# Taking GpSimd out of the first layer's weight conversions, and reordering the loads of weight pieces and alpha, in a retention and two-layer kernel

## The chip, the cores and the metric

The kernel runs on one core of one Trainium2 chip. The metric is the time of one execution in microseconds (us); the median of three runs before the change is 808.59. The engines are called PE (TensorE, the matmuls), PEld (its weight loads), DVE (VectorE), ACT (ScalarE), POOL (GpSimd) and SP (SyncE, which issues the DMAs). L12 is line 12 of the kernel before.

## What is computed

Four batches of 576 tokens pass through a retention with 8 heads of 64 (an attention without softmax, with a decay per head), then through two gated layers:

```python
ret = (q @ k.T / 8) * gamma**(i - j) * (i >= j)        # per head
x = concat_heads(ret @ v)                              # 2304 tokens x 512
h = ((x @ w1) * (x @ w2)) @ w3                         # 512 -> 1024 -> 1024
y = h @ moe_w_out                                      # 1024 -> 512
h = y @ w_in                                           # 512 -> 2048
g = maximum(h, 0) + alpha * minimum(h, 0)              # alpha: one per column of h
out = g @ moe2_w_out                                   # 2048 -> 512
```

The weights of the layers arrive as float64 bits and are converted in the kernel.

## The kernel before

**Numbers.** Each operand of a product is split into a high half (rounded to the matmul's type, by ACT) and a low half (the rest, by a DVE subtraction). A product is then three matmuls: high by high, high by low, low by high.

**A weight piece** (`Weights`, L60 to L144) is 128 x 512 numbers of 64 bits, 512 KB. `_first` makes two ACT passes (L94, L95), `_second` four DVE operations in a row (L104, L105, L107, L109), `_third` the high half (L115), `_fourth` the low half (L123). The subclass `Pieces` (L853) puts `_fourth` on POOL (L858).

**Products** of the first layer, of g and of the output are made by a seven-product scheme for 2 x 2 blocks, so each weight and each third of the tokens also needs sums and differences of its blocks. For the weights w1 and w2 these are four sums of 128 x 256 per column block c (`AbUnits.sums`, L544; for c = 0 on DVE, for the seven others on POOL), for the tokens four subtractions of 128 x 768 (`x_operands`, L599, its `less` in L616; `ab_operands` hands them to POOL), for w_out2 four subtractions of 128 x 256 per pair of pieces (`Operands.add`, L262, its `less` in L271 on POOL). Here the pieces of w_out2 are also multiplied by a sign per row that comes from alpha (`signed`, L287, POOL).

**Stages, in order.**

- *Attention*: one batch is five chunks. Batch 0 runs in two halves, then L707 to L711 lists, step by step, what conversion goes beside which chunk; batches 1 to 3 are 15 links of a chain (L742), and the table `beside` (L724) tells what is put beside each. The order of DVE and POOL is the program's here (L662 to L748), elsewhere a scheduler orders those two; PE, ACT and SP follow the program throughout. `ready` (L674) scales q on POOL (L361, L363) and k on ACT (L354); scores are multiplied by the decay mask on DVE (L388), the state is updated on DVE (L407) and decayed on POOL (L411), and ACT copies the result (L447).
- *Loads of the start* (L649 to L661): SP issues the constants, the pairs of heads of batch 0, and then, between the pairs of batch 1, weight pieces 0 and 1 (`abu.load`). `load_batch(2)` and then piece 2 and 3 (`abu.load(4)`) follow at L712, `load_batch(3)` beside link 4. A raw piece lies in one of three buffers. Alpha is loaded at L831, behind all of it, and L833 to L837 make the sign and its products on DVE.
- *First layer* (L916 to L996): 24 groups, a column block by a third of the tokens, of seven products of six matmuls. Per group ACT copies PSUM four times (L795, L799, L803, L807), DVE reads PSUM three times (L812, L817, L823) and multiplies (L824). A product is often added into a bank that ACT or DVE must have read first. Beside them `at` (L921) places, by group and position a, b or c: the units of w1 and w2, the first ten pieces of w_out1 and w3 (`ws_tick`, spread by `WS`), and pairs of w_out2 (`ops2.tick`, from `OPS0` at `OPS1` tenths), four of eight here (`PAIRS_IN_X`).
- *Fold* (L1027): w3 by w_out1 in 192 matmuls, with the other 14 pieces of these two weights converted beside it.
- *y*: 576 matmuls; w_in is converted beside it, all on DVE and ACT.
- *g* (L1472): 32 groups, a column block by a third of the tokens, as in the first layer but without the units of w1 and w2; the other four pairs of w_out2 are converted at the places listed in `spots` (L1463).
- *Output* (L1577): 18 blocks' worth of seven products each.

Of the kernel before, what the change touches and what calls it, by code (L numbers as in the profile page):

```python
# [12 lines left out]
ALU = mybir.AluOpType  # L13
# [17 lines left out]
WS, OPS0, OPS1 = 24, 43, 10  # L31


def _f32(ap):
    return ap.bitcast(F32)
# [112 lines left out]
def retention_moe_kernel(ctx: ExitStack, tc, qk, kv, w_out1, w3t, w12, w_in, w_out2, alpha, c_row, c_pair, out):  # L148
# [61 lines left out]
    class Operands:  # L210
# [37 lines left out]
        def hi(self, j, u, src):  # L248
            self.u[j, u] = self.places(j, u)
            for h, _, x in self.halves(j, u, src):  # L250
                nc.scalar.copy(h, x)

        def lo(self, j, u, src):
            for h, l, x in self.halves(j, u, src):
                nc.vector.tensor_tensor(out=l, in0=x, in1=_f32(h), op=ALU.subtract)  # L255
            t = self.u.pop((j, u))
            if j != self.stays:
                for n, op in enumerate(self.PLACES[u]):
                    nc.sync.dma_start(out=wod[WOPS.index(op)][:, j].rearrange("p (h w) -> p h w", h=2),
                                      in_=_f32(t[:, n]))  # L260

        def add(self, j, at, steps, ahead=None):  # L262
# [7 lines left out]
            def less(out, a, b):  # L270
                nc.gpsimd.tensor_tensor(out=out, in0=a, in1=b, op=ALU.subtract)  # L271

            def sums1():
                a, b = w.ab[x][0], w.ab[y][0]
                t[1] = self.sum_room(f"t1_{j}").bitcast(F32)
                less(t[1][:, lower], a[:, upper], a[:, lower])
                less(t[1][:, upper], b[:, upper], t[1][:, lower])

            def sums3():
                a, b = w.ab[x][0], w.ab[y][0]  # L280
                t[3] = self.sum_room(f"t3_{j}").bitcast(F32)
                less(t[3][:, lower], b[:, upper], a[:, upper])
                less(t[3][:, upper], b[:, lower], t[1][:, upper])

            def signed(i):
                a = w.ab[i][0]
                nc.gpsimd.tensor_tensor(out=a, in0=a, in1=sg[:, i:i + 1].to_broadcast([P, 512]), op=ALU.mult)  # L287
# [5 lines left out]
                "h1": lambda: self.hi(j, "u1", w.ab[x][0][:, lower]),  # L293
                "l1": lambda: self.lo(j, "u1", w.ab[x][0][:, lower]),
                "h2": lambda: self.hi(j, "u2", w.ab[y][0]), "l2": lambda: self.lo(j, "u2", w.ab[y][0]),
                "t1": sums1, "t3": sums3,
                "h3": lambda: self.hi(j, "u3", t[1]), "l3": lambda: self.lo(j, "u3", t[1]),
                "h4": lambda: self.hi(j, "u4", t[3]), "l4": lambda: self.lo(j, "u4", t[3]),
# [215 lines left out]
    class AbUnits:  # L514
# [203 lines left out]
    def to_xr():  # L718
# [112 lines left out]
    nc.sync.dma_start(out=al, in_=alpha)  # L831

    nc.vector.tensor_scalar(out=sg, in0=al, scalar1=1.0, scalar2=-2.0, op0=ALU.is_gt, op1=ALU.mult)  # L833
    nc.vector.tensor_scalar(out=sg, in0=sg, scalar1=1.0, scalar2=None, op0=ALU.add)
    nc.vector.tensor_tensor(out=sal, in0=sg, in1=al, op=ALU.mult)
    pairs = sg.rearrange("p (j r) -> p j r", r=2)
    nc.vector.tensor_tensor(out=both, in0=pairs[:, :, 0], in1=pairs[:, :, 1], op=ALU.mult)  # L837

    PRE, PAIRS_IN_X = 10, 4
# [116 lines left out]
    at(13, "b", lambda: [ops2.load(i) for i in range(2)])  # L956
# [494 lines left out]
    def come():  # L1451
# [215 lines left out]
```

## Time and profile before

| | us |
|---|---|
| median of 3 runs (806.4 to 809.1) | 808.59 |
| the profiled execution | 807.9 |
| its span, first to last instruction | 806.1 |
| PE busy in the span | 753.7 |
| DVE busy | 649.3 |
| ACT busy | 422.7 |
| POOL busy | 164.2 |
| TensorE's granted clock, mean share of full | 0.981 |

An engine's busy time is the union of its instructions. A matmul's end is modelled, so a busy PE is not PE at its best. The idle time in front of an instruction is put down to what released it last. Of POOL the profile's spans are rough.

### The profile page before, as it was taken

What the parts mean: (1) busy time and instruction counts of PE and PEld (TensorE: products, weight loads), DVE (VectorE), ACT (ScalarE), POOL (GpSimd) and SP (SyncE); (2) the same over time, 40 slices, a digit from 0 to 9 for tenths busy, and PEclk for the clock granted to TensorE, in tenths of its full rate; (3) what the DMA queues carried; (4) which work ended last, traced back from release to release, by engine and by line L of the source; (5) the groups of instructions that cost most, each with busy time, mean ns of one, the idle gap of its engine ahead of it and who ended that gap; (6) DMA issues with size and microseconds to landing.
All of it is one profiled execution on the core that took longest, in us unless ns stands there. A gap on an engine that the chain in (4) does not pass through costs nothing.

```text
span 806.1 us, 13426 instructions
## 1 busy us (share of the span) xinstructions
PE 753.7 (93%) x4979; PEld 701.8 (87%) x4979; DVE 649.3 (81%) x966; ACT 422.7 (52%) x750; POOL 164.2 (20%) x149
## 2 busy tenths in 40 slices
PE   9665899998989989899999999999999999999998
PEld 5555789887988988799999999999999888888887
DVE  4856997999699896989999576979876688777874
ACT  3443465566455553466676554556644454444443
POOL 2344751332245342400000020212010000000000
PEclk9878999999999999999999999999999999999999
DMA  9936014677565696558784698575899944444440
GB/s 355 383 100 229 2 53 164 203 239 253 205 209 186 228 408 242 195 189 320 256 284 165 222 316 318 184 262 193 273 332 348 307 131 131 132 142 132 142 132 27
DMA packets 106849, 173.26 MB, mean 215 GB/s; under 512 B 8096, under 2 KB 73888, under 8 KB 106784
## 3 DMA queue, kind: packets, MB, share of 16 engines
q1 hardware_dynamic: 106784, 172.40, 62.1%
q8 instruction: 39, 0.64, 0.3%
q14 instruction: 26, 0.21, 0.1%
HBM read 112.34 MB, written 60.03 MB: 214 GB/s over the span
## 4 chain that ended last, share of the span: by engine, by line
PE 56%; DVE 11%; DMA 4%; issue 3%; ACT 1%; POOL 0%; SPq 0%; DVEq 0%; ACTq 0%; POOLq 0%
PE h L772 23%; PE o L1379 14%; PE y L1195 12%; PE o L1381 7%; DMA cells<-gd 2%; DVE a L107 2%; DVE a L109 1%; DMA abd<-xs 1%; DVE a L104 1%; DMA raww<-in_w3t_dram 1%; DVE xs L107 1%; DVE xs L255 1%; PE pw L1035 1%; DVE a L105 1%; DVE xs L824 1%
## 5 line engine op out<-in xcount | busy, mean ns | idle before, releaser
L1195 PE MATMUL y<-yab,wa 128*128 128x384 f32 x576 | 100.2, 334 | 0.0
L1195 PEld LDWEIGHTS y<-yab,wa 128*128 128x128 f32 x576 | 99.8, 188 | 0.3 <-DVE yab L1017 0.2
L1360 DVE TENSOR_TENSOR cells<-cells,cells 128x1024 fp32r<-128x1024 f32 x63 | 76.3, 1221 | 26.7 <-ACT cells L1354 26.6
L1379 PE MATMUL o<-wa,cells 128*128 128x512 f32 x288 | 76.6, 393 | 0.0
L1354 ACT CAST cells<-cells 128x1024 fp32r<-128x1024 f32 x63 | 64.9, 1053 | 7.0 <-DVE cells L1347 4.2
L772 PE MATMUL h<-xl,wa 128*128 128x384 f32 x288 | 55.6, 339 | 3.9 <-DVE xs L812 2.3
L1379 PEld LDWEIGHTS o<-wa,cells 128*128 128x128 f32 x288 | 51.4, 189 | 8.5
L1379 PE MATMUL o<-wop,cells 128*128 128x512 f32 x216 | 57.0, 392 | 1.0 <-DVE cells L1391 1.0
L772 PE MATMUL h<-xT,wa 128*128 128x384 f32 x288 | 55.8, 335 | 0.8 <-DVE g L1258 0.7
L772 PE MATMUL h<-xB,wa 128*128 128x384 f32 x288 | 56.5, 334 | 0.0
L772 PE MATMUL h<-wa 128*128 128x384 f32 x264 | 51.4, 343 | 4.8 <-DVE xs L812 2.6
L772 PEld LDWEIGHTS h<-xl,wa 128*128 128x128 f32 x288 | 51.2, 191 | 5.2 <-DVE xs L812 3.0
L287 POOL TENSOR_TENSOR a<-a,al 128x512 f32<-128x512 f32 x8 | 8.8, 1099 | 219.3 <-DVE a L109 219.3
L772 PEld LDWEIGHTS h<-wa 128*128 128x128 f32 x264 | 47.1, 192 | 6.0 <-DVE xs L812 3.2
L772 PE MATMUL h<-xr,wa 128*128 128x384 f32 x240 | 46.9, 341 | 5.1 <-DVE xs L812 3.2
L772 PEld LDWEIGHTS h<-xT,wa 128*128 128x128 f32 x288 | 50.3, 188 | 1.4 <-DVE g L1258 1.4
L772 PEld LDWEIGHTS h<-xB,wa 128*128 128x128 f32 x288 | 50.5, 188 | 0.0
L772 PEld LDWEIGHTS h<-xr,wa 128*128 128x128 f32 x240 | 42.5, 191 | 6.3 <-DVE xs L812 3.9
L1379 PEld LDWEIGHTS o<-wop,cells 128*128 128x128 f32 x216 | 39.4, 188 | 8.9 <-issue 1.2
L109 DVE CUSTOM_DVE_ANT_0 a<-a,b 128x1024 uint16<-128x1024 uint16 x54 | 44.3, 822 | 1.8
L1381 PEld LDWEIGHTS o<-wa,cells 128*128 128x128 f32 x288 | 41.8, 190 | 3.5
L1381 PE MATMUL o<-wa,cells 128*128 128x256 f32 x288 | 44.5, 282 | 0.0
(232 smaller groups left out, 1677.4 us busy)
## 6 DMA issues: line engine op xcount, KB each, us to landing
gd<-g SPq DMA_DIRECT2D x96, 192.0 KB, 4.2
cells<-gd SPq DMA_DIRECT2D x36, 512.0 KB, 6.0
abd<-xs SPq DMA_DIRECT2D x24, 384.0 KB, 3.4
yf<-abd SPq DMA_DIRECT2D x24, 384.0 KB, 6.3
rawi<-in_w_in_dram SPq DMA_DIRECT2D x16, 512.0 KB, 5.7
wod<-xs SPq DMA_DIRECT2D x28, 256.0 KB, 4.0
xs<-in_w_out_dram SPq DMA_DIRECT2D x12, 512.0 KB, 4.9
wa<-wod SPq DMA_DIRECT2D x12, 512.0 KB, 6.4
```

Of the source, the lines that this page charges most:

```text
L104: nc.vector.tensor_scalar(out=a, in0=a, scalar1=self.LEAST, scalar2=self.MOST, op0=ALU.max, op1=ALU.min)
L105: nc.vector.tensor_scalar(out=ai, in0=ai, scalar1=5, scalar2=2, op0=ALU.logical_shift_left, op1=ALU.logical_shift_right)
L107: nc.vector.scalar_tensor_tensor(out=ai, in0=upper, scalar=0xC0000000, in1=ai, op0=ALU.bitwise_and, op1=ALU.bitwise_or)
L109: nc.vector.tensor_tensor(out=a.bitcast(I32), in0=a.bitcast(I32), in1=b, op=ALU.add)
L255: nc.vector.tensor_tensor(out=l, in0=x, in1=_f32(h), op=ALU.subtract)
L287: nc.gpsimd.tensor_tensor(out=a, in0=a, in1=sg[:, i:i + 1].to_broadcast([P, 512]), op=ALU.mult)
L772: nc.tensor.matmul(ps, a[:, x, ks], b[:, y, k], start=(fresh and n == 0), stop=(n == 5), skip_group_check=True)
L1195: nc.tensor.matmul(ys[o], wpc[c][a][:, oc], yab[u][:, bb, c % 2], start=(c == 0 and i == 0), stop=(c == C1 - 1 and i == 2))
L1354: nc.scalar.copy(h.bitcast(F32R), self.q[name])
L1360: nc.vector.tensor_tensor(out=l.bitcast(F32R), in0=q[name], in1=h, op=ALU.subtract)
L1379: nc.tensor.matmul(ps, h[:, k], w[k], start=(fresh and k == 0), stop=(k == C1 - 1), skip_group_check=True)
L1381: nc.tensor.matmul(ps[:, 256:], l[:, k], w[k][:, 0:256], start=False, stop=(k == C1 - 1), skip_group_check=True)
```

## The change

The first layer's POOL work goes to DVE: the sums of w1 and w2, the subtractions of the tokens' blocks for all three thirds, the low halves of w_out1 and w3 (in the fold too), and the subtractions of w_out2. For the pairs of w_out2 that are converted there, the sign is not multiplied in first; it is a scale of the ACT pass and a scalar of the DVE operation. In g these steps stay on POOL, with the sign multiplied as before. Three pairs of w_out2 are converted in the first layer and five in g. Pieces 0 and 1 are loaded ahead of batch 1, alpha and piece 2 behind batch 1 and ahead of batch 2. The steps beside the chunks and links move, and the operations on alpha come beside link 1.

```diff
-WS, OPS0, OPS1 = 24, 43, 10
+WS, OPS0, OPS1 = 29, 49, 10
...
-        def hi(self, j, u, src):
+        def hi(self, j, u, src, sign=None):
             self.u[j, u] = self.places(j, u)
             for h, _, x in self.halves(j, u, src):
-                nc.scalar.copy(h, x)
+                if sign is None:
+                    nc.scalar.copy(h, x)
+                else:
+                    nc.scalar.activation(h, x, AF.Copy, scale=sign)
...
+                    nc.vector.scalar_tensor_tensor(out=l, in0=x, scalar=sign, in1=_f32(h), op0=ALU.mult,
+                                                   op1=ALU.subtract)
...
-            def less(out, a, b):
-                nc.gpsimd.tensor_tensor(out=out, in0=a, in1=b, op=ALU.subtract)
+            late = not self.small
+            sx, sy, sxy = (sg[:, x:x + 1], sg[:, y:y + 1], both[:, j:j + 1]) if late else (None, None, None)
+
+            def less(out, a, b, sign=None):
+                if sign is not None:
+                    nc.vector.scalar_tensor_tensor(out=out, in0=a, scalar=sign, in1=b, op0=ALU.mult, op1=ALU.subtract)
+                else:
+                    (nc.vector if late else nc.gpsimd).tensor_tensor(out=out, in0=a, in1=b, op=ALU.subtract)
...
             def signed(i):
                 a = w.ab[i][0]
-                nc.gpsimd.tensor_tensor(out=a, in0=a, in1=sg[:, i:i + 1].to_broadcast([P, 512]), op=ALU.mult)
+                if not late:
+                    nc.gpsimd.tensor_tensor(out=a, in0=a, in1=sg[:, i:i + 1].to_broadcast([P, 512]), op=ALU.mult)
...
-            engine = nc.vector if c == 0 else nc.gpsimd
+            engine = nc.vector
...
-        return x_operands(p, place, in_sums, nc.gpsimd)
+        return x_operands(p, place, in_sums)
...
-    load_pair(1, 0)
-    abu.load(1)
-    load_pair(1, 1)
-    load_pair(1, 2)
     abu.load(2)
-    load_pair(1, 3)
+    load_batch(1)
+    nc.sync.dma_start(out=al, in_=alpha)
+    abu.load(3)
...
+    def signs():
+        nc.vector.tensor_scalar(out=sg, in0=al, scalar1=1.0, scalar2=-2.0, op0=ALU.is_gt, op1=ALU.mult)
+        nc.vector.tensor_scalar(out=sg, in0=sg, scalar1=1.0, scalar2=None, op0=ALU.add)
+        nc.vector.tensor_tensor(out=sal, in0=sg, in1=al, op=ALU.mult)
+        pairs = sg.rearrange("p (j r) -> p j r", r=2)
+        nc.vector.tensor_tensor(out=both, in0=pairs[:, :, 0], in1=pairs[:, :, 1], op=ALU.mult)
...
-                 ab_steps(0, "f0"), s1[2], ready(rs[1], 0), ab_steps(0, "s0"), s1[3], ready(rs[1], 1), ab_steps(0, "h0 f1"),
-                 s1[4], ready(rs[1], 2), ab_steps(0, "s1 l0"), s1[5], ready(rs[1], 3), ab_steps(0, "h1")):
+                 ab_steps(0, "f0"), s1[2], ab_steps(0, "f1"), s1[3], ready(rs[1], 0), ab_steps(0, "s0"), s1[4],
+                 ready(rs[1], 1), ab_steps(0, "s1 h0"), s1[5], ready(rs[1], 2), ready(rs[1], 3),
+                 ab_steps(0, "l0 h1")):
...
-        0: [ab_steps(0, "l2"), ab_steps(1, "f0")],
-        1: [ready(rs[2], 0), ab_steps(1, "s0")],
-        2: [ready(rs[2], 1), lambda: make.extend(ab_operands(0)), x_steps(1), ab_steps(1, "f1")],
-        3: [ready(rs[2], 2), ready(rs[2], 3, nc.vector), x_steps(1)],
-        4: [lambda: load_batch(3), ab_steps(1, "s1")],
-        5: [x_steps(2)],
+        0: [ab_steps(0, "l2")],
+        1: [signs, ab_steps(1, "f0")],
+        2: [ready(rs[2], 0), lambda: make.extend(ab_operands(0)), x_steps(1), ab_steps(1, "s0")],
+        3: [ready(rs[2], 1), ready(rs[2], 2), ready(rs[2], 3, nc.vector), x_steps(1)],
+        4: [lambda: load_batch(3), ab_steps(1, "f1"), x_steps(1)],
+        5: [x_steps(1), ab_steps(1, "s1")],
...
-    nc.sync.dma_start(out=al, in_=alpha)
...
-    PRE, PAIRS_IN_X = 10, 4
+    PRE, PAIRS_IN_X = 10, 3
...
-        def _fourth(self, i):
-            hi, lo = self.dest.pop(i)
-            nc.gpsimd.tensor_tensor(out=lo, in0=self.ab.pop(i)[0], in1=_f32(hi), op=ALU.subtract)
...
-    spots = ("2a 2b 2c 3a 3b 3c 4a 4b 5a 5b", "8c 9a 9b 9c 10a 10b 10c 11a 11b 11c",
-             "12c 13a 13b 13c 14a 14b 14c 15a 15b 15c", "17c 18a 18c 19a 19c 20a 20b 20c")
+    spots = ("1a 1b 1c 2a 2b 2c 3a 3b 3c 4a", "5a 5b 5c 6a 6b 6c 7a 7b 7c 8a", "9a 9b 9c 10a 10b 10c 11a 11b 11c 12a",
+             "13a 13b 13c 14a 14b 14c 15a 15b 16a 16b", "17b 17c 18a 18c 19b 19c 20b 20c")
```

## Rows read from the trace of the kernel before

**Rows 1.** Busy time of each engine (instructions) by stage, granted clock, DMA

```profile
core 0: us, PE busy (x) PEld busy (x) DVE busy (x) ACT busy (x) POOL busy (x), PEclk, DMA share, GB/s
102.50:301.00 198.50, 182.32 (x1011) 177.50 (x1011) 174.37 (x279) 114.60 (x228) 76.04 (x65) 0.98 0.62 214
301.10:347.50 46.40, 44.21 (x195) 35.98 (x194) 37.36 (x51) 22.67 (x41) 16.79 (x12) 1.00 0.57 203
447.50:622.80 175.30, 173.93 (x998) 172.68 (x997) 134.64 (x219) 95.94 (x175) 24.28 (x24) 1.00 0.81 278
...
0.00:33.00 33.00, 25.70 (x306) 16.07 (x310) 18.25 (x35) 12.77 (x29) 9.38 (x15) 0.97 0.96 358
347.50:447.50 100.00, 100.00 (x578) 99.78 (x577) 93.48 (x165) 65.55 (x116) 0.00 (x0) 1.00 0.68 244
```

**Rows 2.** Waits of PE over the span: us in total, times, longest

```profile
PE h L772 <- DVE xs L812: 9.5, 8, 3.0
PE h L772 <- ACT h L795: 5.7, 4, 2.3
...
PE h L772 <- DVE g L1258: 1.3, 2, 0.7
...
PE pw L1035 <- ACT wa L115: 1.4, 1, 1.4
...
PE pw L1035 <- POOL wa L858: 0.8, 1, 0.8
```

**Rows 3.** Timeline at PE's longest wait of the first layer: start, us, engine, line

```profile
293.85 1.66 POOL L858 TENSOR_TENSOR xl<-a,xl 128x512 fp32r<-128x512 f32 x1 [5.55 <-ACT xl L115]
294.30 1.76 DVE L109 CUSTOM_DVE_ANT_0 a<-a,b 128x1024 uint16<-128x1024 uint16 x1
...
297.38 2.29 PE L772 MATMUL h<-xr,wa 128*128 128x384 f32 x6 [3.00 <-DVE xs L812]
```

**Rows 4.** First layer, DVE and POOL by form: busy us, mean ns

```profile
L824 DVE TENSOR_TENSOR xs<-xs 128x384 f32<-128x384 f32 x23 | 18.7, 813 | 0.1
...
L542 DVE TENSOR_TENSOR wa<-xs,wa 128x512 fp32r<-128x512 f32 x9 | 6.7, 749 | 0.0
...
L616 POOL TENSOR_TENSOR xs<-xs 128x768 f32<-128x768 f32 x5 | 10.6, 2118 | 6.8 <-DVE xl L612 3.9 <-DVE xr L612 2.8
```

**Rows 5.** The same list in the y stage; last, one L824 in the fold's list

```profile
L107 DVE SCALAR_TENSOR_TENSOR a<-rawi,a 128x512 uint32<-128x512 uint32 x16 | 10.9, 689 | 0.3
L109 DVE CUSTOM_DVE_ANT_0 a<-a,b 128x1024 uint16<-128x1024 uint16 x16 | 10.9, 686 | 0.0
L104 DVE TENSOR_SCALAR a<-a 128x512 f32<-128x512 f32 x16 | 6.7, 422 | 1.3 <-ACT a L94 1.1
...
L1149 DVE TENSOR_TENSOR wa<-s,wa 128x512 fp32r<-128x512 f32 x8 | 5.3, 689 | 0.8 <-ACT wa L1143 0.7
...
L1133 DVE TENSOR_TENSOR s<-a 128x256 f32<-128x256 f32 x8 | 3.4, 422 | 0.2
...
L616 DVE TENSOR_TENSOR t_T<-xs 128x768 f32<-128x768 f32 x3 | 2.9, 953 | 0.0
...
L824 DVE TENSOR_TENSOR xs<-xs 128x384 f32<-128x384 f32 x1 | 0.5, 546 | 0.0
```

**Rows 6.** Timeline of the attention, six instructions behind or after its waits

```profile
32.88 0.49 PE L426 MATMUL o<-heads_r,heads_l 64*64 64x64 f32 x8 [2.70 <-ACT xs L447]
...
47.28 0.66 ACT L94 ACTIVATE a<-raw 128x512 f32<-128x512 f32 x1 [8.82 <-DMA raw<-in_w_dram]
...
49.03 0.91 PE L426 MATMUL o<-heads_l 64*64 64x128 f32 x10 [6.98 <-ACT xs L447]
...
59.07 1.16 PE L384 MATMUL sc<-heads_r 64*128 64x128 f32 x16
...
76.41 0.18 DVE L833 TENSOR_SCALAR al<-al 128x16 f32<-128x16 f32 x1 [5.78 <-DMA al<-in_alpha_dram]
...
77.77 1.97 PE L435 MATMUL o<-heads_l,heads_r 128*64 128x128 f32 x16 [3.40 <-DVE heads_l L388]
```

More of the change, by code (lines that the diff above doesn't have):

```diff
@@ L245, in halves, with lo @@
             return [(t[:, :, 0], t[:, :, 1], src)]
-        def hi(self, j, u, src):
+        def hi(self, j, u, src, sign=None):
             self.u[j, u] = self.places(j, u)
             for h, _, x in self.halves(j, u, src):
-                nc.scalar.copy(h, x)
-        def lo(self, j, u, src):
-            for h, l, x in self.halves(j, u, src):
-                nc.vector.tensor_tensor(out=l, in0=x, in1=_f32(h), op=ALU.subtract)
+                if sign is None:
+                    nc.scalar.copy(h, x)
+                else:
+                    nc.scalar.activation(h, x, AF.Copy, scale=sign)
+        def lo(self, j, u, src, sign=None):
+            for h, l, x in self.halves(j, u, src):
+                if sign is None:
+                    nc.vector.tensor_tensor(out=l, in0=x, in1=_f32(h), op=ALU.subtract)
+                else:
+                    nc.vector.scalar_tensor_tensor(out=l, in0=x, scalar=sign, in1=_f32(h), op0=ALU.mult,
+                                                   op1=ALU.subtract)
             t = self.u.pop((j, u))
@@ L267, in add @@
             t = {}
-            def less(out, a, b):
-                nc.gpsimd.tensor_tensor(out=out, in0=a, in1=b, op=ALU.subtract)
+            late = not self.small
[3 more added lines that the diff above has]
+                    nc.vector.scalar_tensor_tensor(out=out, in0=a, scalar=sign, in1=b, op0=ALU.mult, op1=ALU.subtract)
+                else:
+                    (nc.vector if late else nc.gpsimd).tensor_tensor(out=out, in0=a, in1=b, op=ALU.subtract)
             def sums1():
@@ L276, in sums1 @@
                 less(t[1][:, lower], a[:, upper], a[:, lower])
-                less(t[1][:, upper], b[:, upper], t[1][:, lower])
+                less(t[1][:, upper], b[:, upper], t[1][:, lower], sxy)
             def sums3():
@@ L281, in sums3 @@
                 t[3] = self.sum_room(f"t3_{j}").bitcast(F32)
-                less(t[3][:, lower], b[:, upper], a[:, upper])
-                less(t[3][:, upper], b[:, lower], t[1][:, upper])
+                less(t[3][:, lower], b[:, upper], a[:, upper], sxy)
+                less(t[3][:, upper], b[:, lower], t[1][:, upper], sxy)
             def signed(i):
                 a = w.ab[i][0]
-                nc.gpsimd.tensor_tensor(out=a, in0=a, in1=sg[:, i:i + 1].to_broadcast([P, 512]), op=ALU.mult)
+                if not late:
+                    nc.gpsimd.tensor_tensor(out=a, in0=a, in1=sg[:, i:i + 1].to_broadcast([P, 512]), op=ALU.mult)
             parts = {
@@ L292, in add @@
                 "sx": lambda: w._second(x), "sy": lambda: w._second(y),
-                "h1": lambda: self.hi(j, "u1", w.ab[x][0][:, lower]),
-                "l1": lambda: self.lo(j, "u1", w.ab[x][0][:, lower]),
-                "h2": lambda: self.hi(j, "u2", w.ab[y][0]), "l2": lambda: self.lo(j, "u2", w.ab[y][0]),
+                "h1": lambda: self.hi(j, "u1", w.ab[x][0][:, lower], sx),
+                "l1": lambda: self.lo(j, "u1", w.ab[x][0][:, lower], sx),
+                "h2": lambda: self.hi(j, "u2", w.ab[y][0], sy), "l2": lambda: self.lo(j, "u2", w.ab[y][0], sy),
                 "t1": sums1, "t3": sums3,
-                "h3": lambda: self.hi(j, "u3", t[1]), "l3": lambda: self.lo(j, "u3", t[1]),
-                "h4": lambda: self.hi(j, "u4", t[3]), "l4": lambda: self.lo(j, "u4", t[3]),
+                "h3": lambda: self.hi(j, "u3", t[1], sx), "l3": lambda: self.lo(j, "u3", t[1], sx),
+                "h4": lambda: self.hi(j, "u4", t[3], sx), "l4": lambda: self.lo(j, "u4", t[3], sx),
                 "x": lambda: self.load(x + 2), "y": lambda: self.load(y + 2),
@@ L828, in spill @@
             nc.sync.dma_start(out=abd[self.p][:, self.j], in_=self.f)
-    nc.sync.dma_start(out=al, in_=alpha)
[L833 to L837, printed above, removed]
-    PRE, PAIRS_IN_X = 10, 4
+    PRE, PAIRS_IN_X = 10, 3
     fs_raw, fs_a, fs_b = Ring(xs, 12, 4, 4), Ring(xs, 28, 2, 3), Ring(xs, 40, 2, 2)
@@ L955, in retention_moe_kernel @@
         at(m // 3, "abc"[m % 3], ws_tick)
-    at(13, "b", lambda: [ops2.load(i) for i in range(2)])
+    at(15, "b", lambda: [ops2.load(i) for i in range(2)])
     for n in range(7 * PAIRS_IN_X + 1):
```

## The prediction

> **What bounds the kernel now.** I read the stretches first [rows 1]: the attention up to 102.5 us, the first layer (24 groups of 42 matmuls) from 102.5 to 301, the fold of the two weights, then y, the second layer g and the output blocks. g does the same 1008 matmuls as the first layer and takes 175.3 us with TensorE (PE) all but gapless; the first layer takes 198.5. So 23.2 us of the first layer are no matmul time. In y PE never stops either. Time can be won only ahead of 347.5 us: in the attention, the first layer and the fold.
>
> Then the waits of PE [rows 2]. In the first layer they end on two things: VectorE's (DVE) L812, which must have read a PSUM bank before the next product may be added into it, and ScalarE's (ACT) copy L795. Those two make 15.2 us; the rest of the 23.2 is matmuls just after a wait and the clock, which the stretch grants at 0.98 of full against 1.00 in g [rows 1]. L812 itself is short; it is late because DVE works in order behind conversions of weights.
>
> The timeline at the longest of these waits shows why DVE is late [rows 3]: an L109 that starts beside a GpSimd (POOL) operation takes 1.76 us, and PE then idles 3.00. In y, where POOL does nothing, the same L109 takes 0.686 [rows 5]. The list by form tells it for the whole stretch [rows 4]: L824 takes 0.813 on the mean, against 0.546 for one in the fold with no POOL beside it, L542 0.749 against 0.689 for the like L1149 [rows 5]. Subtracting the price of the y stretch, 13 such groups (L824 with 6.1 the largest, L542 with 0.5 among the smallest) were lengthened by 32.5 us together, out of DVE's 174.4 busy [rows 1]. POOL was busy 76.0 there, so each of its microseconds cost DVE 0.43.
>
> In the attention three waits have nothing to do with POOL [rows 6]. ACT stands 8.82 us before L94 of the third weight piece, whose load is queued behind the whole third batch, and PE idles 6.98 behind it. DVE stands 5.78 us before L833 for alpha, queued last of all, and PE idles 3.40. An earlier piece, queued between the pairs of the second batch, leaves PE idle 2.70.
>
> **The change, part by part. First layer.** All POOL work of this stretch goes. DVE gets 24 sums of 128x256 at 0.422 (10.1 us), 5 subtractions L616 at 0.953 (4.8), 12 low halves (the former L858) at 0.689 like L1149 (8.3) and, for three pairs of w_out2, 12 subtractions at 0.422 (5.0): 28.2 us [rows 5]. The 8 multiplications by the sign (L287) vanish: the sign rides in operations that are there anyway, DVE's with a scalar operand at the price of their kind (L107 is one), ACT's as a scale. The fourth pair leaves for g: two conversions at 2 x 0.422 + 0.689 + 0.686 = 2.22, three low halves at 0.689 and one at 0.422: 6.9 less. DVE then has 174.4 - 32.5 + 28.2 - 6.9 = 163.2 us to do. Whether PE waits depends on how full DVE is. It was 174.4/198.5 = 88% full; at the same fullness 163.2 us need 185.8, so the stretch **gains 12.7**. Bounds: 23.2 (no wait left, g's length) and, with PE's waits as frequent as now, 0. I take 12.7, as the same four readers of PSUM per group must still squeeze between conversions. What stands late next is the L812 behind the sums, now four more DVE instructions in a row.
>
> **Attention.** The SP queue now issues two pieces (six DMAs) ahead of the second batch, alpha and the third piece (three DMAs) behind it and ahead of the third. Up to 33 us the queue runs at 358 GB/s [rows 1], so two pieces of 0.52 MB put the first pair of the second batch back by 2.9 us, the middle two by half of it, the last by nothing, since as many bytes stand before it as did. PE needs all four pairs for its next batch, so the 2.70 shrinks by 1.0 at most. The third piece now costs the third batch the 1.5 us that it waited itself: that batch is there by about the time at which the piece came, 47.3, and its first scores now start at 59.07 [rows 6], so some 10 us are free before this load is the next thing late. The waits for piece and alpha go: 6.98 + 3.40 + 1.0 = 11.4. The small operations on alpha move into the ordered part (0.7 us of DVE, like L833). Against it, DVE takes 7 subtractions of 0.953 and 4 sums of 0.422 from POOL, 8.4 us, and gets back 0.43 of the POOL time removed: 7 x 2.12 [rows 4] and 4 of about half of that, 19 us, so 8.2. POOL keeps the scaling and the decay of the states, so stretching does not end there. I take **9** of the 11.4, leaving 2.4 for these and for the order by hand; bounds 0 (the third batch or DVE sets the same pace) and 14.
>
> **Fold.** DVE takes the low halves here too. A piece costs it 2.22 + 0.689 = 2.91 us uncontended [rows 5] and POOL's step leaves the chain. The two waits of PE, 1.4 and 0.8, go [rows 2]: **2.2**; bounds 0 and 46.4 - 44.0 = 2.4.
>
> **g.** A fifth pair is converted here: two loads, seven stores, 10 ACT, 12 DVE and 6 POOL operations, about 7 us of DVE in a stretch where it is busy 134.6 of 175.3 [rows 1]. PE covers it. The steps now also lie where one third of the tokens follows the last, around which both waits of PE (1.3 us for two) lie today [rows 2]. I charge 0.5; bounds 0 and 4 (three such places at 1.3).
>
> **Sum**: 9 + 12.7 + 2.2 - 0.5 = 23.4. The profiled execution spans 806.1 and took 807.9, so 782.7 and 784.5; the median, 808.6, is 0.7 above it: 785. About 0.3% (2.4 us) is what a measurement here can tell from no change.
>
> **Rivals.** *DVE becomes the bound, slower.* If the long rows are not POOL's doing but DMA traffic's or the order's, DVE keeps its 32.5: 174.4 + 28.2 - 6.9 = 195.7, at 88% a stretch of 222.9, 24 us longer, which the 11 of attention and fold do not pay: about 822. It turns slower in this stretch once under 21.3 of the 32.5 come back. For it: DVE is the fullest helper, and L812 behind a queue is the present wait. Against it: y, with DVE 93% busy and POOL at 0, has every price at its minimum [rows 1, 5], and the long ones of rows 3 lie beside POOL. The Trainium skill speaks for it: "Perfetto Trace Analysis", section Optimizing Scalar/DVE Operations, says that where DVE is saturated, handing work to ScalarE or even GpSimd may make sense, and this change does the reverse; the same sentence adds that the two share a read port, so that the hand-over might not help, and the 1.76 beside 0.686 sides with that addition. Chance 0.06.
>
> *Half of it.* Waits shift rather than vanish: the third and fourth batches' loads set the pace of the attention (gain 3) and the four sums in a row keep L812 late (gain 5 in the first layer): 806.1 - 3 - 5 - 2 + 1.8 + 0.7 and 1 for g, about 800. For it: DVE stays 88% full either way. Against: the waits listed sit at the stretched operations. Chance 0.18.
>
> *No effect.* The critical waits are only re-dealt, within 0.3%. For it: PE's slack downstream is nil, but upstream any later load may take over. Chance 0.04.
>
> The forecast, with gains of 15 to 36, has 0.72. Its best case, 14 + 20 + 2, gives 772. The range reaches from there to 800, into the half case, and leaves out about 0.2. **Faster** 0.72 + 0.18 = 0.90, same 0.04, slower 0.06.
>
> **What would show it.** Right: no POOL work between the first group and y; L824 near 0.55 and L109 near 0.69 in every stretch; the first layer about 186 long, its waits for L812 and L795 under 8 us; L94 of the third piece without its 8.82, no wait for alpha, first group near 93.5; g still near 175. Wrong: L824 or L109 still long with POOL idle (then the first rival); DVE over 95% busy in the first layer with more waits for L812; a wait of DVE or ACT for the third batch's loads as long as the one that went; g beyond 178.

## The result, and the profile after

The changed kernel takes 779.02 us (median of 4 runs, 777.58 to 780.67) beside 808.85 for the kernel before on the same chip: a ratio of 0.963, 95% interval 0.960 to 0.967. Forecast were 785 and a range of 772 to 800. The profiled execution took 780.34, its span is 778.6. All lines below are those of the changed kernel; L792 is the former L772, L832 and L844 the former L812 and L824, L815 the former L795. One correction to the text ahead: g has 24 groups, not 32, and the output 9 blocks, not 18; no number rests on these counts.

The windows by stage, columns as in [rows 1]:

```profile
core 0: us, PE busy (x) PEld busy (x) DVE busy (x) ACT busy (x) POOL busy (x), PEclk, DMA share, GB/s
0.00:33.00 33.00, 27.08 (x330) 17.97 (x334) 19.51 (x37) 13.77 (x31) 10.13 (x16) 0.94 0.97 361
33.00:91.50 58.50, 47.43 (x853) 41.29 (x853) 54.95 (x77) 29.00 (x56) 20.81 (x22) 0.86 0.46 171
91.50:271.00 179.50, 177.03 (x1015) 175.07 (x1012) 158.15 (x317) 110.77 (x218) 0.00 (x0) 1.00 0.64 216
271.10:314.60 43.50, 43.50 (x193) 35.99 (x192) 36.02 (x68) 24.78 (x42) 0.00 (x0) 1.00 0.68 247
314.60:414.50 99.90, 99.90 (x578) 99.88 (x577) 92.10 (x163) 65.36 (x116) 0.00 (x0) 1.00 0.67 239
414.50:596.10 181.60, 176.33 (x998) 174.16 (x997) 138.85 (x231) 99.18 (x183) 28.93 (x30) 0.99 0.81 284
```

Subtracted from [rows 1]: the first layer is 19.2 us shorter (198.6 to 179.4, taken between its first and last matmul), the attention 10.8 (102.5 to 91.7), the fold 2.8; y and the output are the same within 0.8; g is 6.3 longer (175.3 to 181.6). POOL stands at 0 from 91.5 to 414.5, PE fills the first layer at a clock of 1.00, and the only place that lost is g.

The list by form of the first layer, to be held against [rows 4] and [rows 5]:

```profile
L837 DVE TENSOR_TENSOR xs<-h,xs 128x384 f32<-128x384 f32 x24 | 13.3, 555 | 12.5 <-PE h L792 12.3
L832 DVE TENSOR_TENSOR xs<-h,xs 128x384 f32<-128x384 f32 x24 | 13.3, 553 | 4.3 <-PE h L792 4.3
L844 DVE TENSOR_TENSOR xs<-xs 128x384 f32<-128x384 f32 x23 | 12.7, 552 | 0.0
...
L109 DVE CUSTOM_DVE_ANT_0 xs<-xs 128x1024 uint16<-128x1024 uint16 x16 | 11.0, 686 | 0.8
...
L109 DVE CUSTOM_DVE_ANT_0 a<-a,b 128x1024 uint16<-128x1024 uint16 x14 | 9.6, 685 | 0.0
...
L123 DVE TENSOR_TENSOR xs<-xs 128x512 fp32r<-128x512 f32 x10 | 6.9, 686 | 0.0
...
L261 DVE SCALAR_TENSOR_TENSOR xs<-xs,al 128x512 fp32r<-128x512 f32 x9 | 6.6, 745 | 1.4 <-ACT xs L254 1.4
```

Every operation that y has too is at y's price again, L109 at 0.686, and the multiplication L844 at 0.552 where it was 0.813. (L261, new in this stretch and with a scalar per row, costs 0.745.) DVE idles 16.8 us in front of L832 and L837 waiting for PE; that is nothing new, before it was 15.0 for the same two operations:

```profile
L817 DVE TENSOR_TENSOR xs<-h,xs 128x384 f32<-128x384 f32 x24 | 13.3, 553 | 11.3 <-PE h L772 11.1
L812 DVE TENSOR_TENSOR xs<-h,xs 128x384 f32<-128x384 f32 x24 | 13.2, 550 | 3.7 <-PE h L772 3.7
```

PE's own waits in this stretch were 15.2 us for L812 and L795 [rows 2]; by the timeline these three are left, 2.5 together:

```profile
143.75 2.37 PE L792 MATMUL h<-xr,wa 128*128 128x384 f32 x12 [0.26 <-ACT h L815]
217.89 2.38 PE L792 MATMUL h<-xl,wa 128*128 128x384 f32 x12 [0.47 <-ACT h L815]
268.84 1.32 PE L792 MATMUL h<-xr,wa 128*128 128x384 f32 x6 [1.74 <-DVE xs L832]
```

In the attention, no wait for the load of the third piece or of alpha is left: L94 of that piece starts without one at 39.88, and so does the first operation on alpha at 40.4. The timelines of ACT and, for g, of ACT and PE:

```profile
39.88 0.68 ACT L94 ACTIVATE a<-raw 128x512 f32<-128x512 f32 x1
...
455.80 0.66 ACT L94 ACTIVATE a<-rawo 128x512 f32<-128x512 f32 x1 [5.13 <-DMA rawo<-in_w_out_dram]
```

```profile
457.56 1.31 PE L792 MATMUL h<-xT,wa 128*128 128x384 f32 x6 [0.27 <-ACT u L1273]
460.71 1.31 PE L792 MATMUL h<-xT,wv 128*128 128x384 f32 x6 [1.84 <-ACT h L1278]
469.11 1.33 PE L792 MATMUL h<-xT,wv 128*128 128x384 f32 x6 [0.84 <-ACT h L1278]
495.57 1.31 PE L792 MATMUL h<-xT,wa 128*128 128x384 f32 x6 [2.01 <-DVE g L1266]
```

A raw piece of g's second pair is what is late now: ACT stands 5.13 before it, ACT's copies behind it come late, and PE waits. PE's waits in g are 5.3 us where they were 1.3; the rest of the 6.3 is matmul time (busy 176.33 beside 173.93), part of it at a lower clock: 0.70 of full from 496 to 498 and 0.50 (the lower of its two levels, 1.2 GHz) from 498 to 500, right behind the last of the four.

### The profile page after: what moved, and what is told of

Its sections match the earlier page's. It is cut to its first block, busy times and chain, and to the rows that moved or that the text cites. A ratio compares the mean times of both kernels' runs of the same rounds, so it can differ in the third digit from the quotient of the medians.

```text
span 778.6 us, 13360 instructions
## 1 busy us (share of the span) xinstructions
PE 750.1 (96%) x4977; PEld 701.6 (90%) x4979; DVE 638.2 (82%) x1042; ACT 424.0 (54%) x750; POOL 59.9 (8%) x67
## 5 line engine op out<-in xcount | busy, mean ns | idle before, releaser
L792 PE MATMUL h<-xT,wa 128*128 128x384 f32 x288 | 55.8, 335 | 2.3 <-DVE g L1266 2.0
L792 PE MATMUL h<-xB,wa 128*128 128x384 f32 x288 | 57.4, 338 | 0.0
L792 PE MATMUL h<-xl,wa 128*128 128x384 f32 x288 | 54.9, 336 | 0.5 <-ACT h L815 0.5
L792 PEld LDWEIGHTS h<-xT,wa 128*128 128x128 f32 x288 | 50.3, 188 | 2.9 <-DVE g L1266 2.3
L792 PEld LDWEIGHTS h<-xl,wa 128*128 128x128 f32 x288 | 50.1, 188 | 1.5 <-ACT h L815 1.4
L792 PEld LDWEIGHTS h<-xB,wa 128*128 128x128 f32 x288 | 51.2, 190 | 0.0
L792 PE MATMUL h<-wa 128*128 128x384 f32 x264 | 49.7, 335 | 0.0
L792 PE MATMUL h<-xr,wa 128*128 128x384 f32 x240 | 45.7, 335 | 2.0 <-DVE xs L832 1.7
L792 PEld LDWEIGHTS h<-wa 128*128 128x128 f32 x264 | 46.0, 188 | 0.3 <-ACT h L815 0.2
L301 POOL TENSOR_TENSOR a<-a,al 128x512 f32<-128x512 f32 x10 | 11.1, 1113 | 444.0 <-DVE a L109 444.0
L792 PEld LDWEIGHTS h<-xr,wa 128*128 128x128 f32 x240 | 41.9, 188 | 2.6 <-DVE xs L832 2.1
L1259 DVE SCALAR_TENSOR_TENSOR g<-h,al,g 128x384 f32<-128x384 f32 x48 | 29.2, 611 | 14.1 <-ACT g L1257 12.0
## 6 DMA issues: line engine op xcount, KB each, us to landing
gd<-g SPq DMA_DIRECT2D x96, 192.0 KB, 4.1
```

Source lines behind the costliest of these rows:

```text
L792: nc.tensor.matmul(ps, a[:, x, ks], b[:, y, k], start=(fresh and n == 0), stop=(n == 5), skip_group_check=True)
L1259: nc.vector.scalar_tensor_tensor(out=g, in0=ps, scalar=sal[:, c], in1=g, op0=ALU.mult, op1=ALU.max)
```

## Experiments

The change has three parts: loads and order of the attention, POOL's work to DVE, and the fourth pair's move with a wider spread of the steps. The first four runs take them apart. Stage lengths in us, each from the kernel's own trace; the totals are medians (the kernel before took 808.54 to 809.55 beside them). Kernels whose attention is that of the changed kernel (e4, e5, e10, e11, e12) end it between 89.5 and 92.7, so differences of one or two microseconds in that column tell nothing:

| kernel | attention | first layer | fold | g | total | ratio to before |
|---|---|---|---|---|---|---|
| before | 102.5 | 198.6 | 46.3 | 175.3 | 808.85 | 1 |
| changed | 91.7 | 179.4 | 43.5 | 181.6 | 779.02 | 0.960 to 0.967 |
| e1_loads | 91.4 | 200.1 | 47.9 | 175.8 | 798.48 | 0.984 to 0.991 |
| e2_engines | 100.6 | 191.5 | 44.4 | 175.8 | 796.09 | 0.982 to 0.989 |
| e3_four | 92.6 | 191.2 | 44.6 | 175.7 | 787.99 | 0.972 to 0.979 |
| e4_g_dve | 89.5 | 179.5 | 43.5 | 181.5 | 778.54 | 0.960 to 0.967 |
| e5_ws24 | 92.7 | 188.3 | 43.6 | 182.4 | 792.01 | 0.975 to 0.982 |
| e6_ws29_four | 91.2 | 192.1 | 43.9 | 174.5 | 786.06 | 0.969 to 0.974 |
| e7_pool_reads | 112.2 | 179.2 | 43.6 | 180.7 | 800.9 | 0.987 to 0.993 |
| e8_pool_writes | 94.6 | 179.4 | 43.5 | 182.7 | 785.4 | 0.965 to 0.974 |
| e9_pool_long | 90.9 | 197.0 | 43.5 | 180.4 | 796.69 | 0.978 to 0.990 |
| e10_spots | 91.8 | 179.3 | 43.6 | 187.0 | 786.2 | 0.966 to 0.976 |
| e11_load_early | 92.5 | 179.3 | 43.5 | 180.5 | 778.68 | 0.957 to 0.967 |
| e12_both | 89.9 | 179.2 | 43.6 | 176.7 | 775.85 | 0.957 to 0.965 |

Where an experiment restores a part of the kernel before, its diff is that part of the change read backwards (with its places of steps); only the marking lines stand here, against the changed kernel.

**The loads alone.**

```diff
-            late = not self.small
+            late = False
...
-            engine = nc.vector
+            engine = nc.vector if c == 0 else nc.gpsimd
...
-        return x_operands(p, place, in_sums)
+        return x_operands(p, place, in_sums, nc.gpsimd)
...
-    PRE, PAIRS_IN_X = 10, 3
+    PRE, PAIRS_IN_X = 10, 4
```

> Only the loads, alpha and the order of the attention's steps as in the changed kernel; the sums, subtractions and low halves stay on GpSimd and w_out2 stays 4 pairs and 4. Theory (two separate gains, the attention's from the loads, the first layer's and the fold's from GpSimd's silence): the first group starts near 92 to 94, the first layer stays near 198, the fold near 46, g near 175; total near 799, 10 under before. Rival (the attention's gain needs VectorE freed from GpSimd too): first group near 98, total near 804.

The attention ends at 91.4, as in the changed kernel, with POOL's work where it was. So the gain of the attention is the loads' and the order's; taking work from POOL there is worth nothing that shows (in the next run, which has only that, the attention ends at 100.6 beside 102.5). The first layer and the fold stay as before, within 1.6.

**The engines alone.**

```diff
-WS, OPS0, OPS1 = 29, 49, 10
+WS, OPS0, OPS1 = 24, 43, 10
...
-    abu.load(2)
-    load_batch(1)
-    nc.sync.dma_start(out=al, in_=alpha)
-    abu.load(3)
+    load_pair(1, 0)
+    abu.load(1)
+    load_pair(1, 1)
+    load_pair(1, 2)
+    abu.load(2)
+    load_pair(1, 3)
...
-    PRE, PAIRS_IN_X = 10, 3
+    PRE, PAIRS_IN_X = 10, 4
```

> Only the engines: everything of the first layer and the fold off GpSimd, sign folded in, 4 pairs and 4, with the loads and the attention's order of before. Theory: first group near 102 as before, first layer near 185 (VectorE has 7 us more to do than with 3 pairs, 165 of it at 88% full gives 187), fold near 43.5, g near 175; total near 794. Rival (the first layer's gain came from its changed places and from the pair that left): first layer near 195, total near 803.

Prices fall at once (the multiplication takes 0.555 on the mean, L109 0.689), but the first layer only goes to 191.5, where 185 to 187 were expected. Freed of POOL, four pairs in their old places still leave PE 10.5 us of waits, and it is the waits for DVE alone that have gone. Those for ACT's copy were 5.7 and are still there [rows 2]; in this run L786 is the former L772, L809 the former L795, L826 the former L812:

```profile
PE h L786 <- ACT h L809: 6.9, 4, 3.4
PE h L786 <- DVE xs L826: 2.3, 1, 2.3
```

**Everything but the fourth pair's move and the spread.**

```diff
-WS, OPS0, OPS1 = 29, 49, 10
+WS, OPS0, OPS1 = 24, 43, 10
...
-    PRE, PAIRS_IN_X = 10, 3
+    PRE, PAIRS_IN_X = 10, 4
...
-    at(15, "b", lambda: [ops2.load(i) for i in range(2)])
+    at(13, "b", lambda: [ops2.load(i) for i in range(2)])
```

> The changed kernel with 4 pairs of w_out2 in the first layer and 4 in g, at the places of before. Theory: g returns from 181.6 to near 175, the first layer grows from 179.5 to near 185, so the total is near that of the changed kernel, 779 plus or minus 2: the moved pair brought nothing. Rival (the first layer has room for the pair, it stays at 180): 773. Rival (the pair had to go, first layer 190 or more): 784.

This is the case of the second rival: the pair had to go. The run splits the first layer's 19.2: engines 7 to 9 (198.6 to 191.5 in e2, 200.1 in e1 to 191.2 here), the move with its spread 11.8. Whether move and spread would gain as much with POOL's work left where it was, no run shows. g returns to 175.7, so the fifth pair costs g 5.9 and the move nets 9 (787.99 to 779.02). The wait at 155.82 shows what is left. PE's timeline, then ACT's and DVE's ahead of it:

```profile
155.82 3.87 PE L792 MATMUL h<-xl,wa 128*128 128x384 f32 x12 [2.61 <-ACT h L815]
...
190.74 3.74 PE L792 MATMUL h<-wa 128*128 128x384 f32 x12 [3.45 <-ACT h L815]
```

```profile
152.87 0.69 DVE L109 CUSTOM_DVE_ANT_0 xs<-xs 128x1024 uint16<-128x1024 uint16 x1
```

```profile
153.65 0.62 ACT L115 CAST xs<-xs 128x512 fp32r<-128x512 f32 x1 [1.48 <-DVE xs L109]
154.17 0.66 ACT L94 ACTIVATE xs<-xs 128x512 f32<-128x512 f32 x1
154.74 0.66 ACT L95 ACTIVATE xs<-xs 128x512 int32<-128x512 uint16 x1
155.30 0.47 ACT L815 COPY h<-h 128x384 f32<-128x384 f32 x1
```

ACT stands 1.48 in front of a piece's L115, because DVE's L109 of that piece has only just been done; two passes of the next piece follow, and only then the copy L815 that PE waits for. The 12 matmuls after that wait take 3.87, where the twelve after the short wait at 217.89 of the changed kernel take 2.38: part of the price of such a wait can be the matmuls behind it. In the next run twelve behind a like wait took 2.37. The granted clock differs: 0.56 of full over the twelve here, 1.00 there (e3_four, then e5_ws24):

```profile
155.80:159.70 3.90, 3.88 (x13) 3.88 (x14) 3.00 (x6) 0.86 (x2) 0.00 (x0) 0.56 0.94 277
155.80:158.20 2.40, 2.35 (x13) 2.35 (x14) 2.33 (x5) 0.89 (x2) 0.00 (x0) 1.00 1.03 392
```

**The spread alone.** `WS` sets the distance of the steps of w_out1 and w3: one every 2.4 positions before, every 2.9 now.

```diff
-WS, OPS0, OPS1 = 29, 49, 10
+WS, OPS0, OPS1 = 24, 49, 10
```

> The changed kernel with the steps of the first ten weight pieces of the fold as close as before (24 tenths instead of 29), pairs still three and five. Theory (with 4 pairs the first layer was 191 for the density of these steps between 140 and 190 us, not for the fourth pair): first layer 187 to 191, total near 788, g unchanged near 181.6. Rival (the fourth pair's amount of VectorE work did it): first layer 179 to 181, total near 779.

One constant costs 8.9 us (179.4 to 188.3), with three pairs. The waits at 155.85 and 189.20 are those of the run before (2.61 and 3.45, both for ACT L815):

```profile
155.85 2.37 PE L792 MATMUL h<-xl,wa 128*128 128x384 f32 x12 [2.61 <-ACT h L815]
...
189.20 3.90 PE L792 MATMUL h<-wa 128*128 128x384 f32 x12 [3.45 <-ACT h L815]
```

**Four pairs and the wide spread.** The four pairs' steps must then follow each other at 8 tenths of a position.

```diff
-WS, OPS0, OPS1 = 29, 49, 10
+WS, OPS0, OPS1 = 29, 49, 8
...
-    PRE, PAIRS_IN_X = 10, 3
+    PRE, PAIRS_IN_X = 10, 4
```

> The changed kernel with 4 pairs of w_out2 in the first layer, started as late as in the changed kernel and therefore packed closer (8 tenths of a place per step), and with the steps of the ten pieces spread as in the changed kernel; in g four pairs at the places of before. Theory (density of the pieces' steps): first layer 181 to 185, with its waits late, where the pairs are packed; g near 175.7; total near 776. Rival (the amount): first layer near 190, total near 786.

The waits near 155 and 190 go and come back later, as 2.89 at 227.77 and 5.93 at 263.61, both for L815; the stretch is 192.1, near the 190 of the rival. In front of the second of them ACT had stood 7.45 before it could write its next half of w_out2, released by the store of an earlier one:

```profile
261.35 0.72 ACT L254 ACTIVATE xs<-xs,al 128x512 fp32r<-128x512 f32 x1 [7.45 <-DMA wod<-xs]
```

So neither is worth much alone. With four pairs the wide spread gains nothing (191.2 to 192.1), with the old spread one pair fewer gains 2.9 (191.2 to 188.3), and both together 11.8. Whether the fourth pair is too much work or its steps are only too close at 8 tenths, this run does not separate; the wait for the store speaks for the second.

**POOL beside DVE, first attempts.** Two runs put idle POOL work into the loop over the groups, on a tile of its own.

```diff
...
+        with tc.manual_schedule(engines={mybir.EngineType.Pool}):
+            for _ in range(2):
+                nc.gpsimd.tensor_tensor(out=pad, in0=pad, in1=pad, op=ALU.subtract)
```

> The changed kernel with 144 GpSimd subtractions of 128x120 on a tile of its own, which nobody waits for, in order from the first group on; nothing else differs. Theory (a GpSimd operation that reads makes VectorE's operations with two inputs in memory wait): while GpSimd runs, L844 and L107 take 1.3 times or more of their 0.55 and 0.68 and PE waits come back there; after it they are short again; total 784 to 795. Rival (GpSimd was only late, it did not slow VectorE): prices and total as in the changed kernel, 779 plus or minus 2.

> The same with 144 GpSimd memsets of 128x120 in place of the subtractions: GpSimd writes and does not read. Theory (it is the reads that meet): operations with two inputs in memory keep their prices (L844 0.55, L107 0.68), the two-speed ones with one input (L104, L105) may be longer; total 778 to 782. Rival (any GpSimd work slows VectorE alike): as with the subtractions, scaled by GpSimd's busy time.

(The second has `nc.gpsimd.memset(pad, 0.0)` in place of the subtraction.) Both missed their place: as nothing held these operations back, POOL issued them from 1.0 us on, ahead of its own work in the attention. The first layer is untouched, 179.2 and 179.4, and says nothing. The attention of the first became 20.5 longer, since POOL's queue is in order and PE then waits for the scaled q and k (18.2 us in eight waits for L376, the former L361; 2.1 in two in the changed kernel); that of the second 2.9. Beside these short subtractions (453 ns on the mean in 65.2 to 76.3) one L109 took 0.758 and one L104 0.611. The attention says something on reads and writes after all, in a few operations. An L631 (the former L616, two inputs in SBUF) takes 1.14 beside the subtractions of e7 and, beside the memsets of e8, the 0.95 that it takes with POOL idle; L109 takes 0.69 beside memsets:

```profile
78.09 1.14 DVE L631 TENSOR_TENSOR xs<-xs 128x768 f32<-128x768 f32 x1
```

```profile
47.63 0.95 DVE L631 TENSOR_TENSOR xs<-xs 128x768 f32<-128x768 f32 x1
```

**POOL beside DVE, in its place.** Here the operand is a piece of a tile that is free only once the tokens of the last third have been read.

```diff
+        if 5 <= n < 15:
+            u = kib(xs, 34, 512)
+            nc.gpsimd.tensor_tensor(out=u, in0=u, in1=u, op=ALU.subtract)
```

> The changed kernel with 30 GpSimd subtractions 128x512 of float32 put into the first layer, on a piece of the xs tile that nothing else reads at that time (three each with groups 5 to 14); nobody waits for them and nothing else runs on GpSimd there. They are about 30 x 1.1 = 33 us of GpSimd. Theory (a long GpSimd operation lengthens VectorE's operations beside it, by 0.43 us for each us of GpSimd, as in the first layer of the kernel before): L844 and L107 take 1.3 times as long or more while GpSimd runs, VectorE gains about 14 us of busy time, PE's waits come back in that stretch, the first layer goes from 179.4 to 184 to 191, the total to 783 to 791. Rival (the lengthening in the kernel before came from something else, for instance from the conversions' operands being wanted by both): VectorE's prices stay at 0.55 and 0.69, first layer 179.4, total 779.

The 30 operations ran in one block from 116.45 on, for 38.85 us. The first layer went from 179.4 to 197.0, beyond what the theory asked, though nobody waits for POOL. DVE and POOL by form in that block, and the windows of the block and the one after it:

```profile
L844 DVE TENSOR_TENSOR xs<-xs 128x384 f32<-128x384 f32 x3 | 4.2, 1391 | 0.0
L107 DVE SCALAR_TENSOR_TENSOR a<-raw,a 128x512 uint32<-128x512 uint32 x2 | 3.0, 1524 | 0.0
L109 DVE CUSTOM_DVE_ANT_0 a<-a,b 128x1024 uint16<-128x1024 uint16 x2 | 2.6, 1290 | 0.0
...
L104 DVE TENSOR_SCALAR xs<-xs 128x512 f32<-128x512 f32 x2 | 2.5, 1260 | 0.0
...
L843 DVE TENSOR_TENSOR xs<-h,xs 128x384 f32<-128x384 f32 x3 | 1.6, 545 | 0.0
L832 DVE TENSOR_TENSOR xs<-h,xs 128x384 f32<-128x384 f32 x3 | 1.6, 545 | 0.0
```

```profile
L978 POOL TENSOR_TENSOR xs<-xs 128x512 f32<-128x512 f32 x30 | 36.6, 1219 | 32.1 <-DVE xl L626 29.8
```

```profile
116.45:155.30 38.85, 28.25 (x140) 27.61 (x139) 36.87 (x38) 12.66 (x26) 36.58 (x30) 0.82 0.43 136
155.30:217.00 61.70, 59.89 (x335) 59.15 (x334) 56.33 (x119) 40.20 (x80) 0.00 (x0) 0.97 0.66 212
```

The changed kernel in the same window:

```profile
116.45:155.30 38.85, 38.59 (x220) 37.83 (x220) 32.61 (x69) 23.87 (x49) 0.00 (x0) 1.00 0.62 200
```

DVE gets 38 operations done beside POOL, 69 without it, and PE 140 matmuls instead of 220. Its L844, L107 and L104 in these lines each take 0.84 us longer than without POOL (0.552, 0.686 and 0.420), while L832 and L843, which read PSUM, keep their 0.55. The 0.84 holds behind another operation from SBUF. Behind one that reads PSUM only 0.37 is added, as with the second of the two L109 whose mean is 1.290:

```profile
132.65 1.52 DVE L109 CUSTOM_DVE_ANT_0 a<-a,b 128x1024 uint16<-128x1024 uint16 x1
...
149.98 0.55 DVE L832 TENSOR_TENSOR xs<-h,xs 128x384 f32<-128x384 f32 x1
150.45 1.06 DVE L109 CUSTOM_DVE_ANT_0 a<-a,b 128x1024 uint16<-128x1024 uint16 x1
```

The difference, 0.47, is what the PSUM operation takes from its start to the next one's. DVE's busy time of the first layer rises by 19.4 (158.1 to 177.4) for POOL's 36.6, 0.53 each. PE waits 4.67 and 5.92 for L832, and its clock is granted at 0.82 in the block. The cause that the forecast read from the trace is thereby shown by itself: POOL's operations alone lengthen DVE's. The Trainium skill, "SBUF — State Buffer", section Who interferes with whom, calls the pair of ports that DVE and GpSimd share an exclusive lock and the only contention between engines; the trace agrees, with ACT's L94 at 0.68 in this block as without POOL.

**g's price.** First, g's pairs off POOL too.

```diff
-            late = not self.small
+            late = True
```

> The changed kernel with the five pairs of g also off GpSimd (subtractions on VectorE, the sign folded in). Theory (g's 5 us of waits come from the fifth pair's load and from conversions queued where one third of the tokens follows the last, not from GpSimd): g stays near 181, between 180 and 183; total within 2 of 779. Rival (GpSimd's lengthening of VectorE makes g's waits too): g near 176, total near 774.

g stays at 181.5 with POOL at 0: POOL is not what the fifth pair costs, as long as the raw piece is late (ACT waits 6.31 for it here). Next, the places of the second to fifth pair, and then the loads.

```diff
-    spots = ("1a 1b 1c 2a 2b 2c 3a 3b 3c 4a", "5a 5b 5c 6a 6b 6c 7a 7b 7c 8a", "9a 9b 9c 10a 10b 10c 11a 11b 11c 12a",
-             "13a 13b 13c 14a 14b 14c 15a 15b 16a 16b", "17b 17c 18a 18c 19b 19c 20b 20c")
+    spots = ("1a 1b 1c 2a 2b 2c 3a 3b 3c 4a", "5c 6a 6b 6c 7a 7b 8b 8c 9a 9b", "9c 10a 10b 10c 11a 11b 11c 12a 12b 12c",
+             "13b 13c 14a 14b 14c 15a 15b 16a 16b 16c", "17c 18a 18c 19a 19c 20a 20b 20c")
```

> The changed kernel with the steps of g's second to fifth pair at later places: the second pair begins at 5c instead of 5a, and the steps after it are spread a little wider, so that its raw piece, loaded at 3c and 4a, is used two places later. Theory (g's 5.9 us are mostly the late raw piece: ScalarE waits 5.13 for it, PE then 0.27 + 1.84 + 0.84 and the clock falls after it, about 3.3 in all; the rest is the last third's x rows, which VectorE waits for, 2.0 + the clock): the waits near 457 to 469 go, the one near 495 may stay, g 181.6 becomes 177 to 179, total 775 to 777. Rival (the fifth pair's own work fills ScalarE and VectorE, and waits turn up elsewhere): g stays at 181 to 182, total 779.

The edit was a poor one: the wait near 457 went, but the third pair now begins right behind its own load (loaded at 9a and 9b, begun at 9c). ACT stands 7.92 before that piece, PE 6.03, and g becomes 187.0. It misses the number and shows the same mechanism at another place. (The expectation has the clock fall behind the waits near 457 to 469; the changed kernel's is 1.00 from 457 to 489 and falls only behind the wait at 495.57.)

```profile
494.94 2.29 PE L792 MATMUL h<-xT,wu 128*128 128x384 f32 x6 [6.03 <-ACT h L1278]
```

```profile
493.29 0.66 ACT L94 ACTIVATE a<-rawo 128x512 f32<-128x512 f32 x1 [7.92 <-DMA rawo<-in_w_out_dram]
```

```diff
-("fx", "sx gx fy", "sy gy", "h1 t1", "l1 h2 t3", "l2 h3", "l3 h4", "l4", "x", "y")
+("fx", "sx gx fy", "sy gy", "h1 t1", "l1 h2 t3", "l2 h3", "l3 h4 x", "l4 y", "", "")
```

> The changed kernel with the raw pieces of g's next pair loaded two places earlier in the pair before (beside its eighth and ninth step instead of its tenth and eleventh). Places of all other steps as in the changed kernel. Theory (the late raw piece costs g about 3.3 us): ScalarE's wait of 5.13 near 455 goes or falls under 2, g becomes 177 to 179, total 775 to 777. Rival 1 (the DMA queues are full there, share 0.95 and above from 456 on, and an earlier issue only lands as late): g 181 to 182. Rival 2 (the piece's place in SBUF is free too late for an earlier load): the issue waits on SP and holds the loads behind it, g 182 or more.

(Counted from one, the two loads move from the ninth and tenth step to the seventh and eighth.) ACT's wait falls from 5.13 to 0.64, and PE's waits for ACT in g go from 3.3 to none; but PE's waits for DVE L1266 grow from 2.0 to 5.0, and g is 180.5. The longest of them, 2.32 at 569.61, is none of the pair's: DVE had stood 3.61 in front of the first operation of the output, for its load (0.39 in the changed kernel):

```profile
566.93 1.23 DVE L1350 TENSOR_TENSOR cells<-cells 128x1024 f32<-128x1024 f32 x1 [3.61 <-DMA cells<-gd]
```

Another, 1.75 at 494.18, is the changed kernel's 2.01 at 495.57, behind the x rows of the last third (here a wait of 1.18 before an L630 that takes 1.34, 0.95 elsewhere). The profiled execution is also the slowest of this kernel's four (781.29, the fastest 776.88), so how much the earlier load alone gives in g stays open.

**Both edits to g.**

> The changed kernel with both of the edits to g that looked a little better by themselves: g's five pairs without GpSimd, and the raw pieces of g's next pair loaded two places earlier. Theory (g's price of 5.9 us is now VectorE's order of work: steps of the extra pair stand in its queue ahead of L1266, L1267 and L1259, which PE's next product waits for; where the piece comes from and which engine takes the sums matters little): PE's waits for DVE L1266 stay at 2 to 6 in all, g 179.5 to 181.5, total 776 to 779, not to be told from the changed kernel. Rival (the two edits add up, since the late piece and GpSimd's slow steps were one chain): g 176 to 178, total 773 to 776.

Neither moved the total alone (778.54 and 778.68 beside 779.02); together they take g to 176.7 in the profiled execution (the fastest of its six), and PE's waits in g to these:

```profile
PE h L792 <- DVE g L1266: 1.4, 2, 1.2
PE h L792 <- ACT h L1278: 0.8, 1, 0.8
```

The 176.7 is what the rival forecast, and it lies outside the 180.4 to 182.7 of the five kernels whose g is the changed kernel's (changed, e5, e7, e8, e9). In g of the changed kernel L1267 takes 0.678 on the mean, here 0.612. That the late piece and POOL's lengthening hid each other, as the rival has it, fits this but is not shown: it rests on one execution, in which ACT still waits 2.58 for the piece, held against the slowest one of e11. The total is 775.85 (774.31 to 780.67, 6 runs); two of the six lie at 780, and the interval overlaps that of the changed kernel, so it is the fastest kernel here by its median and not shown to be faster than the change.

## Why the prediction was right

By its terms, forecast and measured between the two profiled executions (span 806.1 to 778.6, 27.5 against 23.4):

| term | forecast | bounds | measured |
|---|---|---|---|
| attention | 9 | 0 to 14 | 10.8 |
| first layer | 12.7 | 0 to 23.2 | 19.2 |
| fold | 2.2 | 0 to 2.4 | 2.8 |
| g | -0.5 | 0 to -4 | -6.3 |
| y and output | 0 | | 1.0 |

- *Attention.* The two waits went as said; all waits of PE there were 28.2 before and are 16.8. The 2.4 held back for DVE's added work and the order by hand was mostly not needed; e1, with that work still on POOL, gains 11.1.
- *First layer.* The cause was right: long DVE rows are POOL's doing (e9), and the prices fell to those of y. The size was off by 6.5, most of it through DVE's busy time, reckoned at 163.2 and measured at 158.15. The work was reckoned well: the durations of all DVE instructions that start in the stretch add up to 192.0 before and 181.1 after, 10.9 less, and the forecast had 11.2 (operations with the sign as a scalar cost 0.745 where 0.689 was taken, and some steps fell outside the stretch). But durations in a list overlap: at 116.29 in e9 an L564 of 0.42 starts, and the next operation at 116.62. Busy time counts an overlap once, so it is 17.9 less than the sum before and 22.6 less after. The forecast added 53 durations to a busy time, took off 12, and so counted 4.7 us of overlap as work. At its 88% that is 5.3 of the 6.5.
- That the 88% then fits again (158.15 in 179.4) is luck. It held with four pairs (167.1 in 191.2, 87%), but e5 does 158.8 of DVE work in 188.3, 84%, and e2 took 191.5 where the rule gave 187. The step that failed is "whether PE waits depends on how full DVE is". It put both of PE's waits on DVE, and of the 5.7 for ACT's copy L795 the end of POOL's work took nothing: 6.9 in e2 and 6.7 in e3. What the forecast treated as one sum was two effects: POOL's lengthening (7 to 9 us, mostly the waits for L812), and where the steps stand (11.8, mostly the waits for L795). It did not price the wider spread at all, and the spread is what took ACT's L115 out of the way of L815.
- *Fold.* As said; its two waits are gone, and with 2.8 it went a little past the bound of 2.4. With POOL's work left there (e1) it stays at 47.9.
- *g.* The weakest step: "PE covers it", on DVE's busy share of 134.6 of 175.3. The share hid that the pair's raw piece has a fixed place in the queue of loads, in a stretch whose DMA share is 0.81, and that ACT stands behind it in order. 6.3 lie outside the bound of 4, and g at 181.6 is past the 178 that the forecast named as wrong. Of the 6.3, 4.0 are waits; how much of them the late piece causes, how much POOL's lengthening, stays open (e4, e11, e12).
- *Rivals.* The slower one needed long rows with POOL idle; there were none, and DVE stood at 88%. The half case asked that the later batches' loads set the attention's pace and that L812 stay late; neither came (91.7, and 1.7 us of waits for L832).
- *The total.* Its nearness is in part luck. The first layer gave 6.5 more than forecast and g cost 5.8 more, and the two nearly cancel; of the 4.1 by which the sum was short, the rest is 1.8 in the attention, 0.6 in the fold and 1.0 in y and output.

## What to carry to other kernels

Before handing work to a slow engine, look at what the neighbours' rows cost beside it: here 76 us of GpSimd cost VectorE 32.5, and taking the work back on a VectorE 88% full made room. Once no row is long, the position of a step counts as much as the sum of steps: an engine that works in order and waits for a half-finished conversion holds every copy behind it. Do not add listed durations to a busy time: they overlap, and the busy time counts that once. And a busy share says nothing on whether a load arrives in time; follow the load from its issue to its first use before pricing a moved step at nothing.

## What was not expected of the hardware

In e9 a POOL operation of 1.219 us did not slow DVE's by a factor: an operation of 0.420 and one of 0.686 both became 0.84 longer, so the shortest ones tripled (L104, 0.420 to 1.260). DVE finishes about one such operation per POOL operation (29 beside 30), and those that read PSUM pass untouched. That behind one of these only 0.37 is added looks as if DVE waited for what is left of the POOL operation under way. In e7 the length matters too: beside operations of 0.453 an L109 became 0.07 and an L104 0.19 longer, beside a POOL L376 of 1.44 an L566 went from 0.418 to 1.37. In the first layer other lengths were not tried.
